# Forming the x sums of the last layers from two banks of transposed row blocks

## The chip, the cores and the metric

The kernel runs on one core of one Trainium2 chip. The metric is the device time of one execution in microseconds (us). The engines are TensorE (PE: matmuls, with weight loads as PEld), VectorE (DVE), ScalarE (ACT), GpSimd (POOL) and SyncE (SP), which here only issues DMAs. Every engine works through its own list of instructions in order.

## The reference

Attention, a mixture of eight experts and a two-layer network, one after the other; cut to what matters here:

```python
def _moe_ref(x, w_gate, w1, w2):           # x [2304, 512], 8 experts, 1024 hidden
    ...                                    # P: gate probabilities, normalised
    for e in range(E):
        h = np.maximum(x @ w1[e], 0.0)
        ye = h @ w2[e]
        out += P[:, e:e + 1] * ye

def _moe2_ref(x, w_in, w_out):             # 2048 hidden: the "last layers"
    h = x @ w_in
    g = np.where(h > 0.0, h, alpha * (np.exp(np.minimum(h, 0.0)) - 1.0))
    return (g @ w_out).astype(np.float32)

def reference(**kwargs):
    ...
    x = _moe_ref(x=attention_output, **moe_kwargs)
    return _moe2_ref(x=x, **moe2_kwargs)
```

## The kernel before

**Arithmetic.** Each fp32 operand is split into a high part `h` (rounded to fp32r) and the rest `l`; a product is three fp32r matmuls (h·h, l·h, h·l). The first layer of every stage (x times w) is a seven-product scheme: 512 features and the tokens are halved, and `Quad.product` multiplies one of the operands "11", "12", "22", "s1" to "s4" of x with one of w. "s1" to "s4" are sums and differences of x's blocks "11", "12", "21", "22" (first index: half of the features, second: half of the tokens). `keep` (L1048, L1050) and `evac` (L1011) take the products out of the PSUM banks into the hidden tiles `hs`. The second layer (`mix2`, L133 to L137) sums into `accs` on VectorE (L1110) in the mixture.

**Stages.** Attention is followed by the mixture, which goes by units of 512 hidden features: first 1024 tokens (pass 0), then the last 1152 tokens, nine blocks of 128 (pass 1). The loop index is `a`; units 14 to 29 are pass 1. A unit is `mix1` (7 products times 4) and then `mix2_all` (one tile of 128 tokens after the other). The last layers follow, in turns: `k` = 0 to 7 for the first 1024 tokens (p = 2), 8 to 15 for the last 1152 (p = 3). A turn's first layer (steps a, b, z) stands beside the second layer of the turn before (steps t).

**What sets the order.** Everything is written out by hand (`manual_schedule`): the deques `side1` and `side2` hold the work for later (weights to be loaded, split into parts, stored), and a part is popped after each PE step of `mix1` and `mix2_all`. In the last layers the steps of ELU (ACT L1029 to L1031, DVE L1034 and L1035, ACT L1038, POOL L1039) are popped by an estimated clock. PSUM has eight banks, handed out in a ring of six (tag "b") and two. All DMAs go through SyncE's queue.

**The weights of the last layers** come as 64-bit numbers. `weights64_pair` (units in `PAIRS`) and `weights64` (singles, the other units) load them, take them apart on VectorE (`words`, L800 to L805), ScalarE (L814, L828) and POOL (L815), and store their parts.

**The x of the last layers.** `x_rows` turns a block of 128 tokens by four TensorE transposes into one bank, copies it (ACT L874) and stores it to the DRAM tile `xe`: for p = 2 in units 14 and 15 (`BACK`), from rows loaded back from `yd`; for p = 3 in turn 1, from `accs`. `x_operands` then loads a chunk of `xe` (L887, eight blocks at a time), forms the sums (DVE L891), splits them (ACT L904, POOL L908) and stores them to `xo`; a unit in `OPERANDS` does one chunk (unit 25: four), turns 3 to 6 do two each for p = 3. `operands` (L918) loads from `xo` what the products read.

## Time and profile before

| | us |
|---|---|
| median of 3 runs | 2046.77 (2046.49 to 2046.79) |
| the profiled execution | 2047.24 |
| its span in the trace | 2045.5 |

The granted TensorE clock is 0.989 of full speed over the span. In this execution pass 1 begins at 868.36 us from the span's start, and the last layers begin at 1655.70. The starts of the units and turns that the rows name: unit 14 at 868.36, 17 at 1012.48, 18 at 1059.29, 26 at 1451.37, 27 at 1515.29, 29 at 1608.91; turn 0 at 1655.70, 1 at 1663.90, 2 at 1694.90, 3 at 1715.70, 4 at 1737.50, 5 at 1764.20, 8 at 1836.60, and turn 10 at 1885.60. A row of a stretch gives the bounds and the length, then the busy time of each engine with its count of instructions, the granted clock, the busy share of the DMA engines and their GB/s. In a timeline row, the bracket at the end is the engine's idle time ahead of the instruction, and what ended it.

### The profile page before, as it was taken

What the parts mean: (1) busy time and instruction counts of PE and PEld (TensorE: products, weight loads), DVE (VectorE), ACT (ScalarE), POOL (GpSimd) and SP (SyncE); (2) the same over time, 40 slices, a digit from 0 to 9 for tenths busy, and PEclk for the clock granted to TensorE, in tenths of its full rate; (3) what the DMA queues carried; (4) which work ended last, traced back from release to release, by engine and by line L of the source; (5) the groups of instructions that cost most, each with busy time, mean ns of one, the idle gap of its engine ahead of it and who ended that gap; (6) DMA issues with size and microseconds to landing.
All of it is one profiled execution on the core that took longest, in us unless ns stands there. A gap on an engine that the chain in (4) does not pass through costs nothing. (4 is left out here: it accounts for less than half of the span.)

```text
span 2045.5 us, 30595 instructions
## 1 busy us (share of the span) xinstructions
PE 1985.8 (97%) x11099; PEld 1729.0 (85%) x11099; DVE 1520.1 (74%) x2841; ACT 822.9 (40%) x1680; POOL 803.6 (39%) x681
## 2 busy tenths in 40 slices
...
GB/s 234 142 119 212 113 196 62 72 84 97 108 65 96 118 83 72 229 122 90 73 104 128 109 111 107 109 108 83 139 109 109 160 204 211 229 265 153 119 114 67
DMA packets 221782, 262.15 MB, mean 128 GB/s; under 512 B 14016, under 2 KB 167872, under 8 KB 221632
## 3 DMA queue, kind: packets, MB, share of 16 engines
...
HBM read 194.62 MB, written 65.54 MB: 127 GB/s over the span
## 5 line engine op out<-in xcount | busy, mean ns | idle before, releaser
L133 PE MATMUL m<-w2h,hh 128*128 128x512 f32 x1360 | 536.0, 394 | 9.8 <-ACT hh L1038 9.6
L137 PE MATMUL m<-w2h,hl 128*128 128x512 f32 x1360 | 536.9, 395 | 7.3 <-POOL hl L1039 7.3
L135 PE MATMUL m<-w2l,hh 128*128 128x512 f32 x1360 | 534.5, 393 | 0.0
L1017 ACT ACTIVATE hh<-t 128x288 fp32r<-128x288 f32 (+1 forms) x368 | 184.8, 502 | 416.9 <-DVE t L1011 413.0
L137 PEld LDWEIGHTS m<-w2h,hl 128*128 128x128 f32 x1360 | 256.4, 189 | 66.4 <-POOL hl L1039 13.8
L133 PEld LDWEIGHTS m<-w2h,hh 128*128 128x128 f32 x1360 | 256.4, 189 | 60.8 <-ACT hh L1038 13.2
L135 PEld LDWEIGHTS m<-w2l,hh 128*128 128x128 f32 x1360 | 256.4, 189 | 49.1
L1019 DVE SCALAR_TENSOR_TENSOR hl<-t,hh 128x288 fp32r<-128x288 f32 (+1 forms) x368 | 279.9, 761 | 13.2 <-ACT hh L1017 9.5
L129 POOL TENSOR_TENSOR w2l<-w2r,w2h 128x512 fp32r<-128x512 f32 x120 | 164.0, 1390 | 297.4 <-ACT w2h L125 275.4
L1110 DVE SCALAR_TENSOR_TENSOR acc<-m,pr,acc 128x512 f32<-128x512 f32 x247 | 183.0, 745 | 109.2 <-PE m L137 107.8
L1011 DVE TENSOR_TENSOR t<-q,u 128x288 f32<-128x288 f32 (+1 forms) x348 | 182.3, 525 | 60.3 <-PE q L1069 50.1
L1039 POOL TENSOR_TENSOR hl<-eg,hh 128x288 fp32r<-128x288 f32 (+1 forms) x96 | 97.6, 1019 | 246.9 <-ACT hh L1038 198.9
L745 ACT CAST wh<-wt 128x512 fp32r<-128x512 f32 x120 | 69.1, 619 | 227.6 <-POOL wt L741 227.6
L741 POOL TENSOR_TENSOR wt<-w1r,wt 128x512 f32<-128x512 f32 x60 | 89.1, 1486 | 177.5 <-DVE hl L1019 96.0
L741 POOL TENSOR_TENSOR wt<-w1r 128x512 f32<-128x512 f32 x60 | 79.9, 1335 | 164.4 <-DVE hl L1019 121.4
L749 DVE TENSOR_TENSOR wl<-wt,wh 128x512 fp32r<-128x512 f32 x120 | 115.0, 969 | 13.5 <-ACT wh L745 11.6
L1050 DVE TENSOR_TENSOR u<-q,s 128x288 f32<-128x288 f32 (+1 forms) x116 | 61.2, 527 | 84.5 <-PE q L1069 60.0
L1253 DVE TENSOR_TENSOR acc<-m,acc 128x512 f32<-128x512 f32 x119 | 81.1, 686 | 31.1 <-PE m L137 31.0
L815 POOL TENSOR_TENSOR cp<-r,cp 128x512 f32<-128x512 f32 x32 | 44.5, 1390 | 136.5 <-issue 55.1
L1067 PE MATMUL q<-x11h,wh 128*128 128x288 f32 (+1 forms) x232 | 76.5, 330 | 17.0 <-DVE acc L1110 17.0
L1048 ACT COPY s<-q 128x288 f32<-128x288 f32 (+1 forms) x116 | 51.8, 447 | 92.1 <-PE q L1069 92.1
L255 ACT ACTIVATE e<-s,m 128x192 f32<-128x192 f32 (+1 forms) x128 | 55.7, 436 | 79.8 <-DVE m L247 79.2
...
## 6 DMA issues: line engine op xcount, KB each, us to landing
...
```

The costliest lines, as they stand in the source:

```text
L129: e.tensor_tensor(out=lo, in0=src, in1=hi.bitcast(F32), op=ALU.subtract)
L133: nc.tensor.matmul(ps, ah, bh, start=first, stop=False)
L135: nc.tensor.matmul(ps, ah, bl, start=False, stop=False)
L137: nc.tensor.matmul(ps, al, bh, start=False, stop=last)
L741: eng.tensor_tensor(out=t, in0=get(a), in1=get(b), op=op)
L749: eng.tensor_tensor(out=wop[n + "l"], in0=src, in1=wop[n + "h"].bitcast(F32), op=ALU.subtract)
L1011: nc.vector.tensor_tensor(out=t, in0=ps, in1=rest, op=ALU.add)
L1017: nc.scalar.activation(hh, t, AF.Relu)
L1019: late.append(lambda: nc.vector.scalar_tensor_tensor(out=hl, in0=t, scalar=0.0, in1=hh.bitcast(F32), op0=ALU.max, op1=ALU.subtract))
L1039: nc.gpsimd.tensor_tensor(out=hl, in0=g, in1=hh.bitcast(F32), op=ALU.subtract)
L1110: nc.vector.scalar_tensor_tensor(out=accs[i], in0=ps, scalar=scale, in1=accs[i], op0=ALU.mult, op1=ALU.add)
L1253: nc.vector.tensor_tensor(out=accs[i], in0=ps, in1=accs[i], op=ALU.add)
```

## The change

- `x_rows` and `x_operands`, the DRAM tile `xe` and the chunks are gone. `x_pair` takes two blocks of 128 tokens (one of each half of the tokens), turns them into two PSUM banks, and forms from these banks: the high parts (ACT), the rests (DVE), the sums (ACT copy of half a bank, DVE `first` and `second`), the sums' high parts (ACT) and rests (DVE). Six stores put them into `xo`. The rests, which POOL formed, are formed on VectorE.
- For p = 2 four units (15, 17, 19, 21) do a pair each, with one single of the weights; the weight pairs move to 14, 16, 18, 20, 22, 24, 26, 27; units 23 and 25 do two singles each.
- For p = 3 the pairs are (1, 5), (0, 4), (2, 6) beside the second layer of unit 29, and (3, 7) and block 8 alone (its two halves of 64) in turn 0. The second layer of unit 29 takes its tiles in the order 0, 1, 5, 4, 6, 2, 7, 3, 8.
- For p = 3 the second half of the tokens is blocks 4 to 7 and half of block 8, so `hs` holds them in another order of columns, and one of the four ELU splits is made in two pieces. `TURN_B` and `TURN_END` order the second layer's tiles to match.

```diff
-BACK = (14, 15)
-OPERANDS = {17: 1, 19: 1, 21: 1, 23: 1, 25: 4}
-PAIRS = (16, 18, 20, 22, 24, 26, 27, 28)
+BACK = (15, 17, 19, 21)
+PAIRS = (14, 16, 18, 20, 22, 24, 26, 27)
-XORDER = ("11", "21", "12", "22", "s1", "s2", "s3", "s4")
+XORDER = ("11", "12", "21", "22", "s1", "s2", "s3", "s4")
-TURN_B = "a1 a6 t0 a2 t1 z3 t5 a7 a5 t6 a4 b1 t7 b6 b2 t8 a3 t2 b7 t3 b5 t4 b4"
-TURN_END = "z3 t0 t1 t5 t6 t7 t8 t2 t4 t3"
+TURN_B = "a1 a6 t0 a2 t1 z3 t4 a7 a5 t5 a4 b1 t6 b6 b2 t7 a3 t2 b7 t3 b5 t8 b4"
+TURN_END = "z3 t0 t1 t4 t5 t6 t7 t8 t2 t3"
...
-    xe = {p: dram.tile([128, 4, TP[p - 2]], F32, tag=f"xe{p}", name=f"xe{p}") for p in (2, 3)}
-        (p, q): dram.tile([128, 8, 2, TP[p - 2] // 2], F32, tag=f"xo{p}{q}", name=f"xo{p}{q}") for p in (2, 3) for q in "hl"
+        (p, q): dram.tile([128, 16, TP[p - 2] // 2], F32, tag=f"xo{p}{q}", name=f"xo{p}{q}") for p in (2, 3) for q in "hl"
...
-    def x_rows(p, i, src):
...
-    def x_operands(p, c):
...
+    def x_pair(p, j, rows):
+        n = 128 if j < 4 else 64
+        c = slice(j * 128, j * 128 + n)
         s = {}
+        def turned():
+            ps = [psum.tile([128, 4, 128], F32, tag="b", name="x2t") for _ in rows()]
+            for i, r in enumerate(rows()):
+                for k in range(4):
+                    nc.tensor.transpose(ps[i][:, k], r[:, k * 128:(k + 1) * 128], ident)
+            s[1], s[2] = ps if j < 4 else (ps[0][:, :, :64], ps[0][:, :, 64:])
+        def tile_of(tag, rows, dt):
+            t = tmp.tile([128, 512], dt, tag=tag, name="x" + tag, bufs=2)
+            return t[:, :rows * n].rearrange("p (a f) -> p a f", a=rows)
+        def hi():
+            s["h"] = tile_of("s1", 4, F32R)
+            s["g"] = tile_of("u3", 4, F32R)
+            nc.scalar.copy(s["h"], s[1])
+            nc.scalar.copy(s["g"][:, :2], s[2][:, 2:])
         def comb(o, a, b, op):
+            nc.vector.tensor_tensor(out=o, in0=a, in1=b, op=op)
+        def lo():
+            s["l"] = tile_of("u2", 4, F32R)
+            comb(s["l"], s[1], s["h"].bitcast(F32), ALU.subtract)
+            comb(s["g"][:, 2:], s[2][:, 2:], s["g"][:, :2].bitcast(F32), ALU.subtract)
+            for q, t, g in (("h", s["h"], s["g"][:, :2]), ("l", s["l"], s["g"][:, 2:])):
+                nc.sync.dma_start(xo[p, q][:, 0:4, c], t.bitcast(F32))
+                nc.sync.dma_start(xo[p, q][:, 6:8, c], g.bitcast(F32))
         def first():
+            t = s["s"] = raw_tile((8, n), F32, "xsr")
+            nc.scalar.copy(t[:, 6:8], s[2][:, :2])
+            comb(t[:, 4:6], s[1][:, :2], t[:, 6:8], ALU.subtract)
+            comb(t[:, 0:2], s[2][:, 2:], t[:, 6:8], ALU.add)
         def second():
+            t = s["s"]
+            comb(t[:, 2:4], t[:, 0:2], s[1][:, :2], ALU.subtract)
+            comb(t[:, 6:8], s[1][:, 2:], t[:, 2:4], ALU.subtract)
+        def hi_sums():
+            s["k"] = raw_tile((8, n), F32R, "xsh")
+            nc.scalar.copy(s["k"], s["s"])
+        def lo_sums():
+            comb(s["s"].bitcast(F32R), s["s"], s["k"].bitcast(F32), ALU.subtract)
+            for q, t in (("h", s["k"].bitcast(F32)), ("l", s["s"])):
+                nc.sync.dma_start(xo[p, q][:, 8:16, c], t)
+        return [turned, hi, lo, first, second, hi_sums, lo_sums]
     def operands(p, names, c0, c1):
         for n in names:
             for q in "hl":
+                nc.sync.dma_start(xop[n + q][:, :, c0:c1].bitcast(F32), xo[p, q][:, 2 * XORDER.index(n):2 * XORDER.index(n) + 2, c0:c1])
     def layer_one(u, f, names=WORDER):
         for n in names:
...
+            if self.p > 1:
+                self.elu(i, self.fp + 2 * (j - 1), t)
+                return
-            if self.p > 1:
-                self.elu(hh, hl, t)
-                return
-        def elu(self, hh, hl, t):
+        def elu(self, i, fc, t):
...
+            if self.p == 2 or i == 1:
+                to = [(0, self.n, (i - 1) * self.half + self.g0)]
+            elif self.g0 == 0:
+                to = [(0, self.n, HALF + 64)]
+            else:
+                to = [(0, SL - self.g0, HALF + 64 + self.g0), (SL - self.g0, self.n, HALF)]
-                nc.scalar.copy(hh, g)
-                nc.gpsimd.tensor_tensor(out=hl, in0=g, in1=hh.bitcast(F32), op=ALU.subtract)
+                for a, b, c in to:
+                    hh, hl = (hs[q][:, fc, c:c + b - a] for q in "hl")
+                    nc.scalar.copy(hh, g[:, a:b])
+                    nc.gpsimd.tensor_tensor(out=hl, in0=g[:, a:b], in1=hh.bitcast(F32), op=ALU.subtract)
...
-            pre, mid, rest = [(0, range(4))], [], [(1, range(4)), (5, range(4))]
+            pre, mid, rest = [(0, range(4))], [], [(i, range(4)) for i in ((1, 5, 4, 6, 2, 7, 3, 8) if u == U1 - 1 else (1, 5))]
...
-        chunks2 = deque(x_operands(2, c) for c in range(8))
-            nc.sync.dma_start(back[j], yd[:, 2 * j:2 * j + 2])
-        def x_back(i):
-            x_rows(2, i, back[i // 2][:, i % 2])
+            for i in range(2):
+                nc.sync.dma_start(back[j][:, i], yd[:, j + 4 * i])
...
-            elif a in BACK:
-                j = 2 * BACK.index(a)
-                side1.extend([lambda j=j: load_back(j), lambda j=j: load_back(j + 1)])
-                between = [lambda i=i: x_back(i) for i in range(2 * j, 2 * j + 4)]
+            elif a in BACK:
+                j = BACK.index(a)
+                ld, end = weights64(*singles.popleft())
+                side1.extend([lambda j=j: load_back(j), ld])
+                between = x_pair(2, j, lambda j=j: (back[j][:, 0], back[j][:, 1]))
+            elif a > BACK[-1] and singles:
                 (l0, (c0, d0)), (l1, (c1, d1)) = (weights64(*singles.popleft()) for _ in range(2))
                 side1.extend([l0, l1])
                 b1[13:13], b1[9:9], b1[5:5] = [c1], [d0], [c0]
                 end = [d1]
-            for _ in range(OPERANDS.get(a, 0)):
-                ld, ops = chunks2.popleft()
-                between += [ld, None, None, None] + ops
             if not moe:
                 at[1, 3] = lambda: operands(2, (*XUSE, "s4"), 0, HALF // 2)
                 at[2, 3] = lambda: layer_one(0, 0)
                 first = [lambda: operands(2, XUSE, HALF // 2, SL), lambda: layer_one(0, 1, W22[:-1])]
-                side2.extend([lambda: operands(2, ("s4",), HALF // 2, SL), lambda: layer_one(0, 1, W22[-1:])])
+                side2.extend([lambda: operands(2, ("s4",), HALF // 2, SL), lambda: layer_one(0, 1, W22[-1:])] + 8 * [None])
+                xs_ = [x_pair(3, j, lambda j=j: (accs[j], accs[j + 4])) for j in (1, 0, 2, 3)]
+                xs_.append(x_pair(3, 4, lambda: (accs[8],)))
+                side2.extend(xs_[0] + xs_[1] + xs_[2])
+                side2.extend([None] * (35 - len(side2)))
             elif switch:
                 first = [lambda: second_x(("11", "s2", "12", "s3", "s1", "22"))]
                 side2.append(lambda: second_x(("s4",)))
...
-            side2.extend(b1 + end + between + ld2 if a > BACK[-1] else b1 + between + ld2 + end)
+            if moe:
+                side2.extend(b1 + end + between + ld2 if a in BACK else b1 + ld2 + end)
+        def rows_of(p, q, fc, i):
+            c = i * 128 if p == 2 or i < 4 else SL if i == 8 else (i + 1) * 128
+            return hs[q][:, fc, c:c + 128]
-            if (p, u, f) == (2, 0, 0):
-                for j in (8, 4) if i == 4 else (i,):
-                    x_rows(3, j, accs[j])
-            t = slice(i * 128, i * 128 + 128)
-                for _ in three(ps, hs["h"][:, fc, t], hs["l"][:, fc, t], w2s["h"][:, fc], w2s["l"][:, fc], fc == f, fc > f):
+                h, l = (rows_of(p, q, fc, i) for q in "hl")
+                for _ in three(ps, h, l, w2s["h"][:, fc], w2s["l"][:, fc], fc == f, fc > f):
...
-            ops = []
-            if k == 2:
-                work = [x_operands(3, c) for c in range(8)]
-                ops = [None] * 8
-            elif 3 <= k < 7:
-                ops = work[2 * k - 6][1] + work[2 * k - 5][1]
-            if 2 <= k < 6:
-                ops += [work[2 * k - 4][0], work[2 * k - 3][0]]
-            side2.extend(ops)
+            if k == 0:
+                side2.extend(xs_[3] + xs_[4])
```

VectorE at the end of unit 17 of the mixture, before: the rests of the weights (`wl`), the sums into `acc`, and the four sums of a chunk (`xr`).

```order
L805 TENSOR_SCALAR cp<-ct 128x512
L749 TENSOR_TENSOR wl<-wt_10116,wh 128x512
L749 TENSOR_TENSOR wl<-wt_10171,wh 128x512
L1110 SCALAR_TENSOR_TENSOR acc_113<-m_10199,pr,acc_113 128x512
L749 TENSOR_TENSOR wl<-w1r,wh 128x512
L1110 SCALAR_TENSOR_TENSOR acc_115<-m_10224,pr,acc_115 128x512
L891 TENSOR_TENSOR xr<-xr 128x128 x4
L1110 SCALAR_TENSOR_TENSOR acc_116<-m_10245,pr,acc_116 128x512
L1110 SCALAR_TENSOR_TENSOR acc_117<-m_10267,pr,acc_117 128x512
```

After: `xu` and the `xsr` rows are one pair's rests and sums from the two banks `x2t`, and the last of them the rest of the sums, 1024 columns wide.

```order
L803 TENSOR_SCALAR cp<-ct 128x512
L1126 SCALAR_TENSOR_TENSOR acc_111<-m_10221,pr,acc_111 128x512
L890 TENSOR_TENSOR xu_10249<-x2t,xs_10245 128x512
L890 TENSOR_TENSOR xu_10246<-x2t,xu_10246 128x256
L890 TENSOR_TENSOR xsr<-x2t,xsr 128x256 x2
L890 TENSOR_TENSOR xsr<-xsr,x2t 128x256
L890 TENSOR_TENSOR xsr<-x2t,xsr 128x256
L1126 SCALAR_TENSOR_TENSOR acc_113<-m_10262,pr,acc_113 128x512
L890 TENSOR_TENSOR xsr<-xsr,xsh 128x1024
L1126 SCALAR_TENSOR_TENSOR acc_114<-m_10285,pr,acc_114 128x512
L1126 SCALAR_TENSOR_TENSOR acc_115<-m_10299,pr,acc_115 128x512
```

The three `wl` rows and the chunk's sums no longer stand here; the pair's seven instructions stand between the sums into `acc` of the unit's last tiles.

SyncE's queue from the last loads of x (`xs4`) and weights (`wh`, `wl`) of the first turn to the second layer's weights (`w2h`, `w2l`), before:

```order
L918 DMA xs4h<-xo2h 128x2x224
L918 DMA xs4l<-xo2l 128x2x224
L923 DMA wh<-wqh 128x2x128
L923 DMA wl<-wql 128x2x128
L930 DMA w2h<-wdh 128x512
L930 DMA w2l<-wdl 128x512
```

After, the last six of eighteen stores that stand between `wl` and `w2h` (three pairs, the other twelve ahead of these):

```order
L897 DMA xo3h<-xs_16185 128x4x128
L898 DMA xo3h<-xu_16186 128x2x128
L897 DMA xo3l<-xu_16189 128x4x128
L898 DMA xo3l<-xu_16186 128x2x128
L918 DMA xo3h<-xsh 128x8x128
L918 DMA xo3l<-xsr 128x8x128
L937 DMA w2h<-wdh 128x512
L937 DMA w2l<-wdl 128x512
```

The loads of the second layer's weights moved behind the stores of three pairs.

VectorE where unit 29 ends and the last layers begin (`q` is a product of turn 0), before:

```order
L1110 SCALAR_TENSOR_TENSOR acc_115<-m_16143,pr,acc_115 128x512
L1110 SCALAR_TENSOR_TENSOR acc_116<-m_16157,pr,acc_116 128x512
L1110 SCALAR_TENSOR_TENSOR acc_117<-m_16171,pr,acc_117 128x512
L1050 TENSOR_TENSOR u_16209<-q_16202,s_16200 128x512
L1011 TENSOR_TENSOR t<-q_16211,s_16200 128x512
L1050 TENSOR_TENSOR u_16232<-q_16225,u_16209 128x512
L1011 TENSOR_TENSOR t<-q_16234,u_16232 128x512
L1034 SCALAR_TENSOR_TENSOR eg<-eg,er 128x512
L1035 SCALAR_TENSOR_TENSOR eg<-t,eg 128x512
L1011 TENSOR_TENSOR t<-q_16250,u_16232 128x512
```

After:

```order
L1126 SCALAR_TENSOR_TENSOR acc_110<-m_16204,pr,acc_110 128x512
L890 TENSOR_TENSOR xsr<-xsr,xsh 128x1024
L1126 SCALAR_TENSOR_TENSOR acc_115<-m_16221,pr,acc_115 128x512
L890 TENSOR_TENSOR xu_16266<-x2t,xs_16262 128x512
L890 TENSOR_TENSOR xu_16263<-x2t,xu_16263 128x256
L1066 TENSOR_TENSOR u_16280<-q_16273,s_16250 128x512
L890 TENSOR_TENSOR xsr<-x2t,xsr 128x256 x2
L890 TENSOR_TENSOR xsr<-xsr,x2t 128x256
L890 TENSOR_TENSOR xsr<-x2t,xsr 128x256
L1018 TENSOR_TENSOR t<-q_16290,s_16250 128x512
L890 TENSOR_TENSOR xsr<-xsr,xsh 128x1024
L1066 TENSOR_TENSOR u_16323<-q_16316,u_16280 128x512
```

Pieces of the third and fourth pair stand between the last sums into `acc` and between the first sums of turn 0.

## Rows read from the trace of the kernel before

**Rows 1.** the page's part 1: engine, busy time, share, instructions

```profile
PE 1985.8 (97%) x11099; PEld 1729.0 (85%) x11099; DVE 1520.1 (74%) x2841; ACT 822.9 (40%) x1680; POOL 803.6 (39%) x681
```

**Rows 2.** waits of TensorE, whole span: line <- releaser: us in total, times, longest

```profile
PE q L1067 <- DVE acc L1110: 23.1, 6, 6.3
PE m L133 <- ACT hh L1038: 9.6, 7, 3.7
PE m L137 <- POOL hl L1039: 7.3, 13, 1.0
```

**Rows 3.** by stretch: length; PE, PEld, DVE, ACT, POOL busy; PEclk, DMA share, GB/s

```profile
868.36:917.02 48.66, 48.66 (x293) 44.19 (x292) 30.84 (x56) 16.43 (x35) 10.85 (x8) 1.00 0.33 102
1012.48:1059.29 46.81, 46.81 (x277) 42.54 (x276) 40.40 (x68) 17.75 (x36) 24.36 (x18) 1.00 0.36 108
1059.29:1109.74 50.45, 47.31 (x277) 42.60 (x276) 39.88 (x74) 17.30 (x37) 23.83 (x19) 1.00 0.34 109
1451.37:1515.29 63.92, 50.80 (x277) 45.74 (x276) 41.63 (x81) 19.60 (x41) 26.57 (x21) 0.87 0.37 115
1059.29:1515.29 456.00, 431.24 (x2485) 390.85 (x2484) 356.23 (x634) 158.82 (x331) 215.06 (x159) 0.97 0.35 109
1608.91:1655.69 46.78, 46.78 (x277) 42.53 (x276) 26.90 (x51) 11.31 (x25) 11.43 (x9) 1.00 0.97 283
```

**Rows 4.** timeline of VectorE at the end of unit 17: start, us, operation

```profile
1058.83 1.44 DVE L749 TENSOR_TENSOR wl<-w1r,wh 128x512 fp32r<-128x512 f32 x1
1064.74 1.02 DVE L891 TENSOR_TENSOR xr<-xr 128x128 f32<-128x128 f32 x4 [3.81 <-DMA xr<-xe]
```

**Rows 5.** timeline of SyncE's queue there

```profile
1061.87 0.93 SPq L887 DMA_DIRECT2D xr<-xe  x2
```

**Rows 6.** timeline of TensorE after units 17 and 25

```profile
1066.48 0.40 PE L1067 MATMUL q<-x11h,wh 128*128 128x288 f32 x1 [2.26 <-DVE acc L1110]
...
1081.14 0.40 PE L1067 MATMUL q<-xs4h,wh 128*128 128x288 f32 x1 [0.88 <-DVE t L1011]
...
1461.55 0.58 PE L1067 MATMUL q<-x22h,wh 128*128 128x288 f32 x1 [6.05 <-DVE acc L1110]
```

**Rows 7.** VectorE groups by shape: xcount | busy, mean ns | idle before, releaser

```profile
L1050 DVE TENSOR_TENSOR u<-q,s 128x512 f32<-128x512 f32 x36 | 24.8, 690 | 52.8 <-PE q L1069 49.2 <-ACT s L1048 3.6
L1050 DVE TENSOR_TENSOR u<-q,s 128x288 f32<-128x288 f32 x80 | 36.3, 454 | 31.7 <-ACT s L1048 17.5 <-PE q L1069 10.8 <-PE m L137 2.9
```

**Rows 8.** waits of ScalarE, whole span

```profile
ACT r L828 <- POOL cp L815: 82.8, 16, 7.5
```

**Rows 9.** by stretch, as rows 3: turns 0, 1, 2, 4, 3 to 7, 10

```profile
1655.70:1663.90 8.20, 8.20 (x37) 6.76 (x36) 3.95 (x6) 2.89 (x5) 0.00 (x0) 1.00 0.98 318
1663.90:1694.90 31.00, 26.57 (x128) 21.45 (x127) 23.92 (x28) 18.22 (x33) 9.58 (x7) 0.94 0.47 132
1694.90:1715.70 20.80, 20.80 (x92) 16.83 (x91) 14.69 (x21) 10.78 (x18) 3.87 (x3) 1.00 0.80 236
1737.50:1764.20 26.70, 23.45 (x91) 17.72 (x90) 21.10 (x33) 13.97 (x24) 12.15 (x9) 0.94 0.74 219
1715.70:1836.60 120.90, 110.72 (x451) 85.44 (x450) 95.34 (x143) 60.64 (x101) 51.68 (x37) 0.97 0.73 230
1885.60:1909.20 23.60, 23.60 (x141) 21.33 (x140) 19.26 (x38) 14.40 (x36) 7.06 (x9) 1.00 0.42 124
```

**Rows 10.** waits in turn 4

```profile
DVE xr L891 <- DMA xr<-xe: 3.4, 1, 3.4
PE m L133 <- ACT hh L1038: 1.7, 2, 1.0
```

**Rows 11.** timeline of SyncE's queue, end of unit 29: last weight load

```profile
1653.78 0.47 SPq L923 DMA_DIRECT2D wl<-wql  x1
```

**Rows 12.** timeline of VectorE, end of unit 29

```profile
1655.92 0.75 DVE L1110 SCALAR_TENSOR_TENSOR acc<-m,pr,acc 128x512 f32<-128x512 f32 x1 [1.97 <-PE m L137]
```

**Rows 13.** timeline of TensorE in turn 1

```profile
1675.52 0.50 PE L133 MATMUL m<-w2h,hh 128*128 128x512 f32 x1 [3.75 <-ACT hh L1038]
```

More of the change, by code (lines that the diff above doesn't have):

```diff
@@ L866, in weights64_pair @@
         return [c0.load, c1.load], [c0.words, c0.value, c1.words, c1.value], [sums, plain, hi, lo, store]
-    def x_rows(p, i, src):
-        ps = psum.tile([128, 4, 128], F32, tag="b", name="x2t")
-        for j in range(4):
-            nc.tensor.transpose(ps[:, j, :], src[:, j * 128:(j + 1) * 128], ident)
-        t = raw_tile((4, 128), F32, "x2")
-        nc.scalar.copy(t, ps)
-        nc.sync.dma_start(xe[p][:, :, i * 128:(i + 1) * 128], t)
-    def x_operands(p, c):
-        k, g = divmod(c, 4)
-        m = TP[p - 2] // 8
-        s = {}
-        def load():
-            s["x"] = raw_tile((8, m), F32, "xr")
-            src = xe[p].rearrange("p (a k) (h c) -> p k a h c", a=2, h=2)
-            for a in range(2):
-                nc.sync.dma_start(s["x"][:, 2 * a:2 * a + 2], src[:, k, a, :, g * m:(g + 1) * m])
-        def comb(o, a, b, op):
-            x = s["x"]
-            nc.vector.tensor_tensor(out=x[:, o], in0=x[:, a], in1=x[:, b], op=op)
+    def x_pair(p, j, rows):
+        n = 128 if j < 4 else 64
+        c = slice(j * 128, j * 128 + n)
+        s = {}
+        def turned():
[12 more added lines that the diff above has]
+            nc.scalar.copy(s["g"][:, :2], s[2][:, 2:])
+        def comb(o, a, b, op):
+            nc.vector.tensor_tensor(out=o, in0=a, in1=b, op=op)
[6 more added lines that the diff above has]
+                nc.sync.dma_start(xo[p, q][:, 6:8, c], g.bitcast(F32))
@@ L906, in lo @@
-        def lo(o):
-            x, h = s["x"][:, o:o + 4], s["h"][:, o:o + 4]
-            nc.gpsimd.tensor_tensor(out=x.bitcast(F32R), in0=x, in1=h.bitcast(F32), op=ALU.subtract)
-            if o:
-                for q, t in (("h", s["h"].bitcast(F32)), ("l", s["x"])):
-                    nc.sync.dma_start(xo[p, q][:, :, k, g * m:(g + 1) * m], t)
-        return load, [first, lambda: hi(0), second, lambda: lo(0), lambda: hi(4), lambda: lo(4)]
+            t = s["s"]
+            comb(t[:, 2:4], t[:, 0:2], s[1][:, :2], ALU.subtract)
@@ L1212, in tile_net @@
                 side1.append(ld)
-            elif a > BACK[-1] and singles and OPERANDS.get(a) == 1:
+            elif a in BACK:
[4 more added lines that the diff above has]
+            elif a > BACK[-1] and singles:
                 (l0, (c0, d0)), (l1, (c1, d1)) = (weights64(*singles.popleft()) for _ in range(2))
```

9 lines of the change are left out of this document (removed).

## The prediction

> **What bounds the kernel now.** I read the page's busy times first: TensorE is busy for 1985.8 of 2045.5 us [rows 1], so the time can only fall where TensorE waits, some 60 us in all, or runs at its lower clock. The waits of TensorE, read next, name three of them [rows 2]: a first-layer product that waits for a sum into `acc` on VectorE (6 times, 23.1 us), and second-layer matmuls that wait for hidden parts from ScalarE and POOL (9.6 and 7.3 us). Then I cut the span into units and turns. A unit of pass 1 takes 46.81 us when TensorE never stops (unit 17), unit 18 takes 50.45 and unit 26 takes 63.92 [rows 3]. Units 18 to 26 together take 456.00 us, which is 9 x 46.81 = 421.29 and 34.7 more. That excess is in units 18, 20, 22, 24 and 26, each behind a unit that did chunks of x sums. In the last layers turn 2, which has no chunk, takes 20.80 us with TensorE busy throughout; turn 4, with two chunks, takes 26.70, and turns 3 to 7 take 120.90, 16.9 over 5 x 20.80 [rows 9].
>
> The timelines show how a chunk stops TensorE. At the end of unit 17 VectorE reaches the chunk's sums, which wait 3.81 us for the load from `xe` [rows 4] that SyncE issued only at 1061.87 [rows 5]. The last two sums into `acc` stand behind them, so their PSUM banks come free late, and the next unit's product waits 2.26 us for its bank [rows 6]. 15 us later another product waits 0.88 us, and behind the four chunks of unit 25 the first such wait is 6.05 us [rows 6], and the lower clock follows: unit 26 has a mean granted clock of 0.87, and its TensorE work takes 50.80 us where unit 17's takes 46.81 [rows 3].
>
> **The change part by part.** *The chunks of p = 2 go.* No load from `xe` is left on VectorE's way, so all of the excess of units 18 to 26 goes: -34.7 us.
>
> *The pairs of p = 2 come.* A pair's seven VectorE instructions, by the line through the 512 and 288 column forms with one PSUM operand (690 and 454 ns, or 1.05 ns a column [rows 7]): one of 512 columns 0.69, five of 256 at 0.42, one of 1024 at 1.23, together 4.0 us. They stand between the last sums of units 15, 17, 19 and 21. ScalarE's part of the pair stands behind a step of the single's weights that waits for POOL; such waits are 82.8 us in 16, 5.2 on average and up to 7.5 [rows 8], so VectorE will run behind TensorE for a few us at the end of these units. The six 128-token sums that follow can take up some of it, since a tile costs VectorE 0.75 us and TensorE about 2.7 (0.75 + 1.97 idle [rows 12]). The nearest row for what is left over is the small wait of 0.88 us, not the 2.26, since no DMA stands in VectorE's way: 4 x 0.88 = +3.5. The bounds are 0 and what unit 18 loses now, 50.45 - 46.81 = 3.64 each, +14.6. No gain below 0 can come of it, as units without chunks don't stop at all.
>
> *Transposes.* Unit 14 has 16 and takes 48.66, so one is (48.66 - 46.81) / 16 = 0.116 us [rows 3]. Their number does not change; 32 move from units 14 and 15 to four units, 36 from turn 1 to unit 29 and turn 0: 0.
>
> *The chunks of p = 3 go* from turns 2 to 6. VectorE waits 3.4 us for a load of `xr` in turn 4, and TensorE's waits there come behind it, through the hidden parts [rows 10]. Turn 2 shows what such a turn takes without them: -16.9. The bounds are -18 (turn 2 is not quite free of work either) and -12, as the elu steps in these turns may keep small waits of their own.
>
> *The pairs of p = 3* go into a place where VectorE is idle 1.97 of every 2.7 us [rows 12] and is busy 26.90 of 46.78 [rows 3], so its time alone costs nothing. Three other things there do.
> First the banks: the transposes of the third and fourth pair wait for a sum into `acc` that has just begun. I take 2 us each, less than the 2.7 of a tile: +4.
> Second the stores. The DMA engines are 97% busy in unit 29 and 98% in turn 0, at 283 and 318 GB/s [rows 3, 9], and SyncE issues the last load of turn 0's weights at 1653.78 [rows 11]. The pairs' stores stand behind it. A pair is 14 rows of 128 x 128 x 4 bytes, twice: 1.84 MB or 5.8 us at 318 GB/s. Three pairs end at about 1671.5, the second layer's weights (8 x 262 KB, 6.6 us) at 1678, and the fourth pair's stores at 1684. The pairs keep their parts in the tiles "s1", "u2" and "u3", two of each, which the products of turn 0 need too: u3 of turn 0 waits until the fourth pair's is stored. Until then the bank of product 5 is not emptied, and step z3 of turn 1, three products into that turn (1663.90 + 4 + the 4 above, or 1672), waits for it: +12.
> Third, the elu of turn 0 begins that much later, and the wait of 3.75 us for the hidden part in turn 1 [rows 13] grows to about 8: +4. Stalls this long bring a stretch at the lower clock; by turn 4 against turn 2 that is 23.45 - 20.80 = 2.6 us of TensorE time [rows 9]: +2.6.
> Together +22.6. The low bound is +8, the banks and the longer elu wait alone, if the stores land before they are needed. The high bound takes every set of stores in full: 4.5 x 5.8 + 4 + 2.6 = +33.
>
> *The split of the elu's last step* adds 16 short copies on ScalarE and as many subtractions on POOL. In turn 10 TensorE is busy 23.60 of 23.60, ScalarE 14.40 and POOL 7.06 [rows 9], so both have room; if that cover is gone, a copy of about 0.4 us in each of eight turns is some 3 us. The other order of tiles and columns moves nothing: 0.
>
> **Sum.** 2047.24 (the profiled execution) - 34.7 + 3.5 - 16.9 + 22.6 = 2021.7. The median of the runs stands 0.47 below the profiled execution: 2021.
>
> **The rivals.** *(a) The start of the last layers costs little*: the stores land in time and only the +8 is left. For it: the queue is at 132 GB/s in turn 1 [rows 9], so there is room once the loads are through. Against: the same row begins with the stall that u3 would lengthen, and nothing lets a store past the loads. 2021 - 14.6 = 2007.
>
> *(b) VectorE becomes the bound of the four units.* The rests of x (0.69 + 0.42 + 1.23 = 2.3 us a pair) move from POOL to VectorE, busy 40.40 of 46.81 in unit 17 where POOL is busy 24.36 [rows 3]. For it: a subtraction took 1.44 us beside POOL's work [rows 4], twice what I put for its width. Against: even with all 4.0 us on top VectorE has 44.4 of 46.81. Each of the four units then loses what unit 18 loses now: + 4 x (3.64 - 0.88) = 2032. The Trainium skill ("Perfetto Trace Analysis", section "Optimizing Scalar/DVE Operations") speaks for this rival: where VectorE is saturated, it says, some of its work may better go to Scalar or even GpSimd, and here it goes the other way (it adds that GpSimd and VectorE share a read port, so that the move between these two might not help). By that rule the time is 2032; the trace has VectorE near saturation only at the end of a unit, so I follow the row.
>
> *(c) The waits of turns 3 to 7 are the elu's own*, not the chunks'. For it: what TensorE waits for there is a hidden part from ScalarE [rows 10]. Against: turn 2 has the same elu and no wait. The 16.9 stay: 2038.
>
> *(d) Slower: the four units stop as unit 26 does now.* The high parts of a pair wait on ScalarE behind POOL, VectorE waits for them with the unit's last sums behind it, and no bank comes free for the next unit's products. For it: the wait of up to 7.5 us [rows 8]. Against: four pairs take the place of eight chunks, so a pair stands for two chunks, half of unit 25's four, and none waits for a load from `xe`. At unit 26's price of 63.92 - 46.81 = 17.1, four units add 4 x (17.1 - 0.9) = 65: 2086. It decides the sign from (25.6 / 4) + 0.9 = 7.3 us a unit.
>
> *(e) The change does not do what it says*, and the stalls come from the weights' steps in the same units: about 2047, as now.
>
> **How the numbers follow.** Forecast 0.48, (a) 0.24, (b) 0.10, (c) 0.08, (d) 0.07, (e) 0.03. The range leaves out (d), (e) and most of (c), 0.17 in all: its low end is (a) with no wait left in the four units (2007 - 3.5 = 2003), its high end (b) with some 3 us for the split, 2035. A measurement of this kernel can tell about 0.2%, 4 us, from no change. Faster is all but (d) and (e): 0.90; same is (e): 0.03; slower is (d): 0.07.
>
> **What would show it.** Units 18 to 26 near 9 x 46.81 = 421 us, with at most a short wait in 16, 18, 20 and 22, show the first two steps right; waits over 2 us there, behind a sum on VectorE, show (b), and over 7 (d). Turns 3 to 7 near 104 us show the fourth. Turns 0 and 1 together take 39.2 us now: near 59 (2.8 us of transposes less, as 24 are in unit 29, and 22.6 more), with a wait of z3 that VectorE's `u3` ends and that one behind a DMA from SyncE's queue, shows the stores' step right; near 44, (a). If the transposes moved to unit 29 cost more than 0.116 us each, or the pairs' pieces hold TensorE in unit 29 itself, the term of the banks was wrong.

## The result, and the profile after

The changed kernel takes 2012.71 us (median of 4 runs, 2011.39 to 2014.66), the kernel before 2046.78 beside it. The ratio is 0.9831, 95% interval 0.9814 to 0.9848: some 34 us less. The forecast was 2021, with a range of 2003 to 2035.

The profiled execution took 2012.12 us and has a span of 2010.3, 35.2 less than before. The first lines of its page, to be read against [rows 1], and the waits of TensorE over the span (line <- releaser: us in total, times, longest), against [rows 2]:

```profile
span 2010.3 us, 30549 instructions
PE 1971.1 (98%) x11099; PEld 1719.9 (86%) x11099; DVE 1521.4 (76%) x2840; ACT 815.8 (41%) x1683; POOL 761.6 (38%) x665
```

```profile
PE q L1083 <- DVE t L1018: 10.4, 1, 10.4
PE m L131 <- ACT hh L1054: 8.2, 1, 8.2
```

The six waits for a sum into `acc` (23.1 us) are gone from the list. What is left are two waits that did not exist at this size before, both in turn 1. By stretch (length, busy time of each engine, granted clock, share and rate of the DMA engines, as [rows 3]), the changed kernel has units 14 to 28, unit 29, turn 0, turn 1, turns 3 to 7, and turn 8 to the end:

```profile
868.33:1574.13 705.80, 705.80 (x4173) 641.31 (x4172) 578.36 (x1012) 256.68 (x537) 313.05 (x232) 1.00 0.34 105
1574.13:1624.91 50.78, 49.73 (x302) 44.95 (x300) 34.32 (x69) 16.18 (x36) 5.54 (x4) 1.00 0.90 265
1624.91:1634.48 9.57, 9.57 (x49) 7.93 (x48) 5.01 (x9) 2.75 (x5) 0.00 (x0) 1.00 0.98 282
1634.48:1677.77 43.29, 24.58 (x91) 18.84 (x91) 28.31 (x41) 19.38 (x34) 8.96 (x7) 0.76 0.68 201
1698.63:1803.86 105.23, 105.09 (x451) 83.69 (x450) 81.69 (x111) 51.13 (x85) 29.01 (x21) 1.00 0.51 168
1803.86:2010.30 206.44, 201.56 (x1159) 179.72 (x1157) 164.71 (x310) 115.33 (x293) 59.67 (x83) 1.00 0.37 114
```

TensorE is busy in all 705.80 us of units 14 to 28, at the full clock. Turn 1 is the opposite: 24.58 of 43.29 us at a mean granted clock of 0.76. The same cut of five kernels (us; the last three are experiments below, and each boundary is the start of the stretch's first matmul):

| stretch | before | changed | p = 2 half alone | p = 3 half alone | `deferred5` |
|---|---|---|---|---|---|
| up to unit 14 | 868.4 | 868.3 | 868.6 | 869.3 | 869.8 |
| units 14 to 28 | 740.5 | 705.8 | 705.8 | 740.0 | 705.8 |
| unit 29, turns 0 and 1 | 86.0 | 103.6 | 86.4 | 109.7 | 80.2 |
| turns 2 to 7 | 141.7 | 126.1 | 141.3 | 126.2 | 130.8 |
| turn 8 to the end | 208.9 | 206.4 | 208.6 | 206.4 | 206.4 |
| span | 2045.5 | 2010.3 | 2010.7 | 2051.5 | 1992.9 |

So the difference of -35.2 is -34.7 in the mixture, +17.7 at the start of the last layers, -15.6 in turns 2 to 7 and -2.5 after them. (A correction to the description of the kernel ahead of the prediction: in the names of x's blocks the first index is the half of the tokens and the second the half of the features. Nothing in the working hangs on it.)

The stall at the start of the last layers, on VectorE: step `keep` of the third product sum in turn 0 ("u<-q,u"), then TensorE at step z3 and at the first second-layer tile.

```profile
1632.77 0.68 DVE L1066 TENSOR_TENSOR u<-q,s 128x512 f32<-128x512 f32 x1
...
1645.75 0.69 DVE L1066 TENSOR_TENSOR u<-q,u 128x512 f32<-128x512 f32 x1 [8.37 <-DMA xo3l<-xu]
```

```profile
1649.09 0.80 PE L1083 MATMUL q<-xs4h,wh 128*128 128x512 f32 x1 [10.35 <-DVE t L1018]
...
1661.71 0.80 PE L131 MATMUL m<-w2h,hh 128*128 128x512 f32 x1 [8.16 <-ACT hh L1054]
```

VectorE waits 8.37 us until the fourth pair's tile `xu` is stored; z3 waits 10.35 us for its bank; and the elu, that much later, makes the next tile wait 8.16 us where it waited 3.75 [rows 13]. On SyncE's queue the first of the pairs' stores, the first of the second layer's weights and the first store of the fourth pair are issued as follows:

```profile
1614.79 0.41 SPq L897 DMA_DIRECT2D xo3h<-xs  x1
...
1632.26 1.38 SPq L937 DMA_DIRECT2D w2h<-wdh  x1
...
1638.39 0.38 SPq L897 DMA_DIRECT2D xo3h<-xs  x1
```

Three pairs take 17.5 us of the queue (17.3 were worked out), and a store issued at 1638 to 1641 holds the tile that VectorE wants at 1637.

In the mixture, unit 17 ends like this on VectorE (a pair's first instruction, its sums, its last):

```profile
1053.58 0.69 DVE L890 TENSOR_TENSOR xu<-x2t,xs 128x512 fp32r<-128x512 f32 x1 [1.97 <-ACT xs L886]
1054.19 0.41 DVE L890 TENSOR_TENSOR xu<-x2t,xu 128x256 fp32r<-128x256 f32 x1
1055.04 0.76 DVE L890 TENSOR_TENSOR xsr<-x2t,xsr 128x256 f32<-128x256 f32 x2 [0.44 <-ACT xsr L902]
...
1057.83 1.23 DVE L890 TENSOR_TENSOR xsr<-xsr,xsh 128x1024 fp32r<-128x1024 f32 x1 [0.46 <-ACT xsh L913]
1058.97 1.40 DVE L1126 SCALAR_TENSOR_TENSOR acc<-m,pr,acc 128x512 f32<-128x512 f32 x2
```

The wait of 1.97 us for ScalarE is there, and the pair's instructions last what the two-point line gave (0.69, 0.42 and 1.23 us). VectorE is done with the unit's sums 3 us after TensorE, and TensorE does not wait for it.

### The profile page after: what moved, and what is told of

Its sections match the earlier page's. It is cut to its first block, busy times and chain, and to the rows that moved or that the text cites. A ratio compares the mean times of both kernels' runs of the same rounds, so it can differ in the third digit from the quotient of the medians.

```text
span 2010.3 us, 30549 instructions
## 1 busy us (share of the span) xinstructions
PE 1971.1 (98%) x11099; PEld 1719.9 (86%) x11099; DVE 1521.4 (76%) x2840; ACT 815.8 (41%) x1683; POOL 761.6 (38%) x665
## 5 line engine op out<-in xcount | busy, mean ns | idle before, releaser
L1055 POOL TENSOR_TENSOR hl<-eg,hh 128x288 fp32r<-128x288 f32 (+2 forms) x112 | 101.7, 915 | 310.6 <-ACT hh L1054 230.2
L747 DVE TENSOR_TENSOR wl<-wt,wh 128x512 fp32r<-128x512 f32 x120 | 107.2, 904 | 12.8 <-ACT wh L743 11.0
L1083 PE MATMUL q<-xs4h,wh 128*128 128x288 f32 (+1 forms) x232 | 75.9, 327 | 10.4 <-DVE t L1018 10.4
L316 PEld LDWEIGHTS o<-vw,pt 112*128 112x128 f32 x512 | 76.7, 193 | 9.1 <-issue 3.9
```

The costliest lines, as they stand in the source:

```text
L747: eng.tensor_tensor(out=wop[n + "l"], in0=src, in1=wop[n + "h"].bitcast(F32), op=ALU.subtract)
L1055: nc.gpsimd.tensor_tensor(out=hl, in0=g[:, a:b], in1=hh.bitcast(F32), op=ALU.subtract)
L1083: nc.tensor.matmul(ps, wh, xh, start=k == 0 and i != 3, stop=False, skip_group_check=True)
```

## The experiments

**One half at a time.** The two halves of the change touch different stretches, so each was run alone. Only the p = 2 half:

> Only the p = 2 half of the change (pairs in units 15, 17, 19, 21; the x of p = 3 as before, through xe and chunks). Theory: the excess of units 18 to 26 (34.7 us) is all that this half touches, and the changed kernel's gain of 34 us is this half alone, while its p = 3 half costs about as much at the start of the last layers as it brings in turns 3 to 7. Expected: units 18 to 26 take 421 us, turns 0 and 1 39 us and turns 3 to 7 121 us as before, time 2012 us. Rival: both halves bring a part of the 34 us, or the halves need each other (the chunks of p = 3 stall on what the pairs of p = 2 left behind): time 2020 to 2035 us.

Measured: 2013.16 us (2012.49 to 2013.65; ratio to before 0.9825, interval 0.9810 to 0.9839), the changed kernel's time. The theory holds: units 14 to 28 take 705.8, and the rest is as before (table).

Only the p = 3 half:

> Only the p = 3 half of the change (pairs in unit 29 and turn 0, order of columns and tiles; the x of p = 2 through xe and chunks as before). Theory: units 18 to 26 keep their 456 us; in turn 1 step z3 waits some 10 us and the first second-layer tile some 8 us, turns 3 to 7 take 105 us and the turns of p = 3 some 2.5 us less, which sums to +17.7 - 15.7 - 2.5 = about 0: time 2044 to 2049 us. Rival: the waits of turn 1 come from the p = 2 half (its other layout of xo, read at the end of unit 29), not from the pairs of p = 3: then turn 1 takes some 27 us here and the time is near 2029 us.

Measured: 2054.04 us (2052.61 to 2055.99; 1.0025, interval 1.0016 to 1.0035). The stall of turn 1 is there, so it comes from the p = 3 pairs; the rival falls. But the time is outside what the theory gave: unit 29 with turns 0 and 1 takes 109.7 us, 6.0 more than in the changed kernel. SyncE's queue shows the difference. Here the weight pair of unit 28 (before, `PAIRS` ends in 28; after, in 27) still stores its parts at the start of unit 29, in front of everything:

```profile
1612.07 1.48 SPq L865 DMA_DIRECT2D wqh<-r  x3
...
1615.17 0.49 SPq L865 DMA_DIRECT2D wqh<-r  x1
...
1655.24 0.41 SPq L947 DMA_DIRECT2D xo3h<-xs  x1
```

Unit 29 begins at 1609.32 in this run, so the first store of a p = 3 pair goes out 45.9 us into it. In the changed kernel it goes out at 1614.79 - 1574.13 = 40.7. What follows is seen in this run: a pair's piece on VectorE waits 4.12 us for an earlier pair's store (at 1659.76), a later pair's transposes wait 3.06 us for the sum into `acc` behind it, and a product waits 1.42 us for a store. So the moved weight pair, which looked like bookkeeping of the p = 2 half, is the likely cause of these 6 us; no run moved it alone.

**The load in front of the sums, in the kernel before.** This asks whether the chunks stalled TensorE by their work or by their load. In the kernel before, the load of [rows 5] stands in SyncE's queue behind a store of the single's parts, which leaves at 1061.45:

```profile
1061.45 0.32 SPq L832 DMA_DIRECT2D wdl<-cp  x1
```

The edit puts the load ahead of the step that issues this store (and drops the three empty steps behind the load, so that the sums come a little earlier too):

```diff
-                between += [ld, None, None, None] + ops
+                if OPERANDS[a] == 1:
+                    b1.append(ld)
+                    between += ops
+                else:
+                    between += [ld, None, None, None] + ops
```

> The kernel before with one edit: in units 17, 19, 21 and 23 the chunk's load from xe is issued ahead of the single's last step (and so ahead of that step's store, which stands in SyncE's queue until POOL is done), not behind it. Theory: the waits of units 18, 20, 22 and 24 (3.64, 4.12, 5.78 and 4.06 us, 17.6 in all) come of VectorE standing in front of a load that is issued late; with the load early they fall to 0 to 1 us each, unit 26 keeps its 17.1 us: 2030 to 2034 us. Rival: the chunk's work, or ScalarE and POOL behind the single, is what keeps VectorE behind: the waits stay at 2 us or more each: 2038 to 2047 us.

Measured: 2036.63 us (2035.99 to 2038.72; 0.9946, interval 0.9931 to 0.9961), between the two. Units 18, 20, 22 and 24 by stretch:

```profile
1059.17:1107.00 47.83, 47.08 (x277) 42.57 (x276) 40.90 (x74) 16.70 (x36) 23.87 (x19) 1.00 0.35 110
1153.81:1204.90 51.09, 47.31 (x278) 42.58 (x277) 41.83 (x74) 16.69 (x36) 23.55 (x19) 1.00 0.32 103
1251.70:1299.49 47.79, 47.06 (x278) 42.56 (x276) 40.90 (x74) 16.68 (x36) 23.88 (x19) 1.00 0.34 110
1346.30:1394.06 47.76, 47.04 (x277) 42.56 (x276) 40.87 (x74) 16.70 (x36) 23.86 (x19) 1.00 0.35 110
```

Three of the four fall to 1.0 us over 46.81, with the same work in them, and VectorE no longer waits for a load in front of the sums, so there the load was the cause. Unit 20 keeps 4.3 us, of another sort: ScalarE waits for the expert's next weights.

```profile
1168.85 0.62 ACT L125 CAST w2h<-w2r 128x512 fp32r<-128x512 f32 x1 [4.86 <-DMA w2r<-in_w_dram]
```

Their load is issued at 1160.74, right behind the chunk's last store, which waits for POOL. The chunk's stores do in the next unit what its load did in its own.

Unit 26, which holds 17.1 of the 34.7 us, is out of reach of this edit and takes 63.6 us here too. For it there is no run, but the trace of the kernel before shows the same order three times at the end of unit 25: the next chunk's load stands behind the store of the chunk before, which waits for POOL, and VectorE waits 7.0 us for each of the three loads.

```profile
1451.04 1.02 DVE L891 TENSOR_TENSOR xr<-xr 128x128 f32<-128x128 f32 x4 [7.00 <-DMA xr<-xe]
...
1459.72 1.02 DVE L891 TENSOR_TENSOR xr<-xr 128x128 f32<-128x128 f32 x4 [6.99 <-DMA xr<-xe]
```

```profile
1454.77 0.52 SPq L911 DMA_DIRECT2D xo2l<-xr  x1
1455.33 1.83 SPq L887 DMA_DIRECT2D xr<-xe  x2
```

**The margin in the four units.** The same pairs, two each in units 17 and 21:

```diff
-                j = BACK.index(a)
...
-                side1.extend([lambda j=j: load_back(j), ld])
-                between = x_pair(2, j, lambda j=j: (back[j][:, 0], back[j][:, 1]))
+                side1.append(ld)
+                if BACK.index(a) % 2:
+                    for j in (BACK.index(a) - 1, BACK.index(a)):
+                        side1.append(lambda j=j: load_back(j))
+                        between += x_pair(2, j, lambda j=j: (back[j][:, 0], back[j][:, 1]))
```

> The changed kernel with two p = 2 pairs each in units 17 and 21 and none in 15 and 19 (same work in all), to see how near the edge one pair is. Forecast's view: VectorE has no slack left at the end of a unit with one pair (a wait of 0.9 us was expected there and none came), so a second pair, 4.0 us of VectorE and 2 to 3 us of waits for ScalarE, makes TensorE wait 3 us and more in units 18 and 22: unit 18 takes 50 us or more, the time is 2018 to 2030 us (with the lower clock behind). Other view: the pairs' steps are spread over a unit's tiles and cost nothing until VectorE's busy time itself passes 46.8 us of the unit: no wait, 2012 to 2014 us.

Measured: 2019.36 us, one run. Units 18 and 22 by stretch:

```profile
1057.85:1106.61 48.76, 47.81 (x278) 42.70 (x277) 41.67 (x77) 17.48 (x37) 19.29 (x15) 1.00 0.45 139
1248.88:1298.07 49.19, 47.81 (x277) 42.70 (x276) 41.65 (x77) 17.47 (x37) 19.28 (x15) 1.00 0.45 138
```

They lose 2.0 and 2.4 us, no more, and the clock stays full. One pair costs nothing, two cost some 2 us: the edge lies between. Neither expectation fits; the stalls are there, as the first view had it, but smaller. (Units 14 to 28 are 4.3 us longer in all, and the first view's time is met only with 2.8 us more in unit 29 and turns 0 and 1, at 106.4, which the edit does not touch.)

**VectorE or POOL for the rest of the sums.** Rival (b) of the prediction:

```diff
-            comb(s["s"].bitcast(F32R), s["s"], s["k"].bitcast(F32), ALU.subtract)
+            (nc.gpsimd if p == 2 else nc.vector).tensor_tensor(out=s["s"].bitcast(F32R), in0=s["s"], in1=s["k"].bitcast(F32), op=ALU.subtract)
```

> The changed kernel with the rest of a p = 2 pair's sums (lo_sums, 1.23 us a pair on VectorE) given back to POOL. Theory: VectorE is not the bound of these units, so nothing changes: 2011 to 2014 us. Rival (b) of the prediction: VectorE near saturation keeps the units at their edge; then the changed kernel would have shown waits there, and this form would be faster than it by up to 1 us a unit. A third way: POOL is later with the next unit's weights, and waits of 1 to 3 us appear in units 16, 18, 20 and 22: 2016 to 2025 us.

Measured: 2014.10 us (2012.71 to 2016.24; 0.9829, interval 0.9813 to 0.9846). Units 14 to 28:

```profile
871.82:1577.63 705.81, 705.81 (x4174) 641.30 (x4172) 573.79 (x1008) 256.74 (x537) 323.49 (x236) 1.00 0.34 105
```

The same 705.8 us with TensorE never idle. VectorE has 4.6 us less to do and POOL 10.4 more, and neither is felt.

**What the start of the last layers waits for: a place in the queue, or the rate.** The stores of the p = 3 pairs from another queue, first ScalarE's, then POOL's (`nc.sync` to `nc.scalar` or `nc.gpsimd` in `x_pair` for p = 3):

> The changed kernel with the six stores of each p = 3 pair issued from ScalarE's queue, not from SyncE's. Theory: in the changed kernel the stores stand in SyncE's queue behind the loads of turn 0 and 1, and the tiles s1, u2 and u3, which the products of turn 0 need again, come free only when they have landed. Then here the wait of z3 in turn 1 (10.4 us) falls under 3 us and the time to 2000 to 2004 us. Rival: the DMA engines are full at that time (97% busy) and the queue does not matter, or the banks held by the transposes are the cause: the wait stays at 8 to 10 us, the time at 2010 to 2013 us, and the loads of turn 0 may come late besides.

Measured: 2023.49 us (2021.64 to 2024.08; 0.9874, interval 0.9859 to 0.9888), slower than either theory gave. The wait of z3 fell to 3.92 us, but ScalarE now stood in front of its own stores, and with it the parts of the next pair and the copies of turn 0:

```profile
1637.34 0.39 ACT L887 CAST xu<-x2t 128x256 fp32r<-128x256 f32 x1
1639.43 0.37 ACTq L897 DMA_DIRECT2D xo3h<-xs  x1
1644.04 0.43 ACTq L898 DMA_DIRECT2D xo3h<-xu  x1
...
1645.89 0.37 ACT L902 COPY xsr<-x2t 128x256 f32<-128x256 f32 x1 [8.16 <-DMA xo3h<-xs]
```

So this run does not separate the two, and POOL was tried, which has nothing else to do in unit 29 and turn 0.

> The changed kernel with the stores of the p = 3 pairs issued from POOL's queue; POOL is idle in unit 29, while ScalarE, which issued them in the run before, had the pairs' high parts behind its stores. Theory (the stores' place in SyncE's queue is what is waited for): they go out from 1609 us on, beside the loads; u3 of turn 0 waits under 4 us instead of 8.4, z3 of turn 1 under 5 instead of 10.4, and unit 29 with turns 0 and 1 takes 90 to 98 us instead of 103.6. Rival (the rate of the DMA engines is what is waited for, whatever the queue): the loads of turn 0 are as much later as the stores are earlier, and unit 29 with turns 0 and 1 takes 101 us or more.

Measured: 2011.55 us, one run. Unit 29 with turns 0 and 1, and the wait of VectorE in turn 0:

```profile
1574.28:1677.16 102.88, 84.84 (x439) 72.49 (x438) 68.98 (x117) 38.41 (x74) 38.10 (x41) 0.90 0.78 242
```

```profile
1642.37 0.69 DVE L1066 TENSOR_TENSOR u<-q,u 128x512 f32<-128x512 f32 x1 [5.77 <-DMA xo3l<-xu]
```

The stores go out from 1609 on, and the wait is still 5.77 us; z3 waits 6.84, the first tile 9.95, the stretch 102.9 against 103.6. The stretch is as the rival had it; the two waits lie between the two views. The place in the queue was worth 2.6 us at VectorE (8.37 before) and 3.5 at z3, and no more: the fourth pair's stores are issued 7 us earlier (1631.16 against 1638.39), but now beside the weights of turn 1 (from 1633.64 on, against 1652.73). That the full DMA engines (share 1.02 and 324 GB/s from 1625.00 to 1634.50) took the rest is argued from this, not tried. The loads of turn 0, which the rival had late, are not: the last is issued at 1614.88, against 1614.22. The first tile then gave 1.8 us back, since POOL's part of the elu stood behind two of the new issues on POOL, and ScalarE waited 2.04 us for it:

```profile
1649.04 0.94 POOL L918 DMA_DIRECT2D xo3h<-xsh  x1 [3.87 <-ACT hh L1054]
1649.97 0.89 POOL L918 DMA_DIRECT2D xo3l<-xsr  x1
1650.87 1.27 POOL L1055 TENSOR_TENSOR hl<-eg,hh 128x512 fp32r<-128x512 f32 x1
```

The Trainium skill ("DMA: Bandwidth & Descriptors", section "Rules for kernel authors") says that spreading DMAs over SP, ACT and GpSimd does not help bandwidth, since they all run on the same 16 DMA engines and only issue time is saved; over the stretch the run agrees, with 0.8 us gained of 17.7.

**Less to store.** If the amount is the cause, the cure is to move the pairs. `deferred` stores the nine blocks of `acc` (2.4 MB instead of 8.3 MB), loads two of them back (`rows_back`) and forms a pair in each of turns 2 to 6:

```diff
+            if not moe:
+                for i in (0, 1, 5, 4, 6, 2, 7, 3, 8):
+                    nc.sync.dma_start(ye[:, i], accs[i])
...
-            if k == 0:
-                side2.extend(xs_[3] + xs_[4])
+            if 1 <= k < 7:
+                ops = []
+                if k > 1:
+                    turned, hi, lo, one, two, *sums = x_pair(3, k - 2, lambda j=k - 2: [back[j][:, i] for i in range(2 if j < 4 else 1)])
+                    ops = [turned, lambda hi=hi, lo=lo: (hi(), lo()), lambda one=one, two=two: (one(), two())] + sums
+                side2.extend(ops + [None] * (14 - len(ops)))
+                if k < 6:
+                    side2.append(lambda j=k - 1: rows_back(j))
```

> The changed kernel with the p = 3 pairs moved: unit 29 only stores its nine blocks of acc to DRAM (2.4 MB, not 8.3 MB of stores), and turns 2 to 6 load two blocks back and form one pair each; the low part of the first blocks goes into a tile of the raw ring. Theory: with 3.5 times less to store at the start of the last layers and no shared tile waiting for it, unit 29 and turns 0 and 1 take some 82 us (85.98 before, less 36 transposes at 0.116), not 103.6; turns 2 to 6 take 0.93 us more each for their transposes: 1994 to 2000 us. Rival: a pair is too much for a turn of 21 us on VectorE or in the banks, and turns 2 to 6 take 23 to 27 us as with the chunks before: 2006 to 2020 us.

Measured: 2008.37 us (2008.28 to 2008.81; 0.9802, interval 0.9787 to 0.9817). Half of each: unit 29 with turns 0 and 1, and turn 2:

```profile
1574.07:1656.90 82.83, 78.00 (x404) 67.28 (x403) 51.40 (x82) 28.02 (x54) 14.71 (x11) 0.96 0.78 235
1656.90:1681.38 24.48, 22.17 (x99) 17.57 (x98) 17.95 (x29) 11.78 (x20) 4.04 (x4) 1.00 0.70 207
```

The start is at 82.8 us (82 expected): with the pairs gone from it, the loss is gone. The edit takes away the bytes to be stored, the pairs' work and their hold on the shared tiles all at once; which of the bytes and the tiles counts was not tried apart (the same stores from tiles of their own would tell). Turns 2 to 5 take 24.5 to 26.3 us, as the rival had it. VectorE shows why:

```profile
1668.24 1.22 DVE L891 TENSOR_TENSOR xsr<-xsr,xsh 128x1024 fp32r<-128x1024 f32 x1 [2.43 <-ACT xsh L914]
1669.38 0.68 DVE L1019 TENSOR_TENSOR t<-q,u 128x512 f32<-128x512 f32 x1
```

The rest of the sums waits for its high part on ScalarE, and behind it stands the elu's first step. That high part and rest were put five and eight steps later:

> The deferred form with the sums' high part and rest (hi_sums, lo_sums) five and eight steps later in turns 2 to 6. In the deferred run TensorE waited some 1.7 and 0.7 us in each of these turns for a hidden part, and VectorE stood 2.4 us in front of lo_sums, which waited for hi_sums on ScalarE, with the first step behind product z3 after it. Theory: that place alone costs the 2.6 us a turn; turns 2 to 6 take 21.8 to 22.2 us instead of 24.5: 1994 to 1998 us. Rival: a pair's 4 us on VectorE are too much for these turns wherever they stand: 24 us and more a turn: 2006 to 2009 us.

Measured: 2028.57 us (2027.79 to 2030.43; 0.9905, interval 0.9889 to 0.9922). Turns 2 and 3:

```profile
1658.20:1680.22 22.02, 21.91 (x100) 17.65 (x98) 16.77 (x28) 11.58 (x20) 3.54 (x4) 1.00 0.63 191
1680.22:1709.98 29.76, 23.66 (x100) 18.96 (x98) 19.70 (x30) 12.30 (x21) 5.45 (x5) 0.89 0.59 177
```

Turn 2 takes the 22.0 us of the theory, so the work fits. Turns 3 to 6 wait for rows. On SyncE's queue the last store of the pair now stands in front of the next pair's load:

```profile
1682.80 0.36 SPq L919 DMA_DIRECT2D xo3l<-xsr  x1
1683.21 1.75 SPq L1285 DMA_DIRECT2D yr<-ye  x2
```

```profile
1687.69 1.51 PE L877 MATMUL x2t<-ident,yr 128*128 128x128 f32 x6 [5.92 <-DMA yr<-ye]
```

It is the fault of the kernel before again: a load behind a store that waits for an engine. `deferred3` has the products a5 and a4 ahead of the first tile in turn 1 besides:

```diff
-TURN_1 = "a1 a6 a2 z3 a7 t4 a5 t5 a4 t6 t7 t0 t1 t2 t3"
+TURN_1 = "a1 a6 a2 z3 a7 a5 a4 t4 t5 t6 t7 t0 t1 t2 t3"
```

> deferred2 with the order of turn 1 changed: the products a5 and a4 ahead of the first second-layer tile t4. Theory: the wait of 4.6 us in front of t4 is the length of the elu of turn 0, and two products of 1.4 us each put in its place cover 2.7 us of it: 2 to 3 us less than deferred2. Rival: the same wait comes back a step later, since ScalarE and VectorE then do the elu of a5 and a4 at the same time: within 1 us of deferred2.

Measured: 2025.39 us (2024.89 to 2026.05; 0.9889, interval 0.9874 to 0.9904), 3.2 less than `deferred2`, as expected. Then the load ahead of the store:

```diff
-                    ops += [None] * 5 + sums[:1] + [None] * 3 + sums[1:]
+                    ops += [lambda j=k - 1: rows_back(j) if j < 5 else None] + [None] * 4 + sums[:1] + [None] * 3 + sums[1:]
```

> deferred2 with the load of the next pair's rows issued right after the pair's sums are formed, not at the turn's end. In deferred2 turn 2 took 22.0 us as expected, but turns 3 to 6 waited 5.9 us each in front of the transposes for rows whose load stood in SyncE's queue behind the store of lo_sums, which VectorE finishes late in the turn. Theory: with the load ahead of that store all of turns 2 to 6 take 22.0 us: 2028.6 less 4 x 7.8 = 1997 us. Rival: the load then waits for its raw tile instead, and the wait in front of the transposes stays above 2 us: 2006 us or more.

Measured: 1995.88 us (1994.81 to 1997.22; 0.9743, interval 0.9729 to 0.9758). Turns 2 to 5 take 22.0 to 22.1 us each. With the order of turn 1:

> deferred4 with the products a5 and a4 of turn 1 ahead of t4, as in deferred3, which was 3.2 us under deferred2. Theory: the same 3 us here, 1994 us. Rival: the gain was one of the two runs' scatter: within 1 us of deferred4.

Measured: 1994.08 us (1993.80 to 1994.65; 0.9734, interval 0.9720 to 0.9749). The medians differ by 1.8 us, and unit 29 with turns 0 and 1 by 2.7 (82.9 and 80.2):

```profile
1575.61:1655.77 80.16, 77.57 (x403) 67.16 (x402) 50.84 (x80) 27.88 (x54) 14.64 (x11) 0.98 0.80 243
1655.77:1765.52 109.75, 109.10 (x487) 87.73 (x486) 95.78 (x146) 59.37 (x104) 25.93 (x20) 1.00 0.70 207
```

This form is faster than both kernels; TensorE is busy in 109.1 of 109.75 us of turns 2 to 6.

## Why the prediction was right, and where its terms were off

- **The chunks of p = 2 (-34.7).** Measured -34.75 over units 14 to 28, with nothing left. That the load was the cause and not the work is shown by `early_load` for three units of four, and for unit 26 by the three waits of 7.0 us in the trace; no run tried that unit.
- **The pairs of p = 2 (+3.5, bounds 0 to 14.6).** Measured 0. The price of a pair was right (4.0 us) and so was the wait for ScalarE (1.97 us; ScalarE itself waits 4.5 us for POOL there). The mis-sized step is what of it reaches TensorE: I took the small wait of 0.88 us as the nearest row, but two pairs in a unit were needed to bring waits of 0.4 to 0.5 us. Rival (b) fell with `lo_pool`: VectorE or POOL made no difference. So the sentence of the Trainium skill ("Perfetto Trace Analysis", section "Optimizing Scalar/DVE Operations") on offloading a saturated VectorE has nothing to act on here: at 40 of 46.8 us it is busy but not saturated.
- **The pairs of p = 3 (+22.6, bounds 8 to 33).** Measured 103.64 - 85.99 = +17.7, by the mechanism that was put: 8.37 us of VectorE in front of a store, 10.35 us at z3 (12 put), 8.16 instead of 3.75 at the first tile (+4.4; 4 put). TensorE's own work in turn 1, without its 36 transposes of before, went from 26.57 - 4.2 = 22.4 to 24.6, +2.2 at the lower clock (2.6 put). The term that was most off is the banks: one wait of 1.05 us ahead of a transpose, where I had put two of 2. Unit 29 itself is held by no more than that; its 24 transposes cost 0.123 us each (49.73 - 46.78 over 24), not 0.116. Turns 0 and 1 together take 52.9 us, between the 59 of the forecast and the 44 of rival (a), and the wait of z3 behind a store decides for the forecast's mechanism. The working had the stores wait for a place behind the loads *and* priced them by the rate; `pool_queue` gives the place 2.6 to 3.5 us of the two waits and 0.8 us of the stretch, and `deferred` shows the whole loss go with the pairs, without parting their bytes from their tiles.
- **The chunks of p = 3 (-16.9).** Measured -15.7 in turns 3 to 7: 105.23 us, 21.0 a turn and not 20.8, with 0.14 us of idle time. Rival (c) fell: the hidden parts come in time once the chunks are out of ScalarE's and POOL's way.
- **Order of tiles and the split (0).** Turn 8 to the end took 2.5 us less, in both kernels that have the p = 3 half (206.4 against 208.6 to 208.9). TensorE's two waits for hidden parts ahead of the last turn's last tiles (0.75 and 0.32 us) are gone, and turn 9 takes 23.5 us instead of 24.3; together 1.9 of the 2.5. I put the order at nothing without looking which tile came behind which hidden part. That the order did it is argued from these places; no run changed the order alone.

The sum came out 9 us too high: two costs were put too high (by 3.5 and 4.9), a gain was left out (2.5), and another gain was put too high (by 1.2). The view behind it, that the two halves of p = 3 nearly cancel, is measured in the changed kernel as +17.7 - 15.6 - 2.5 = -0.4. Alone, with the weight pair of unit 28 in its old place, that half makes the kernel slower by 0.25%.
